# One addition on VectorE, moved behind a tile's lower parts in one step of each unit

## The chip, the core and the metric

The kernel runs on one core of a Trainium2 chip. TensorE (PE, with its weight loads shown as PEld) multiplies and transposes, VectorE (DVE), ScalarE (ACT) and GpSimd (POOL) work beside it, and SyncE (SP) issues the transfers. Each engine takes its instructions in the order of its own queue and waits for others by semaphores. The metric is the device time of one execution in microseconds, lower is better.

## The reference

Attention with a threshold, then two matrix products with a softplus between them. Eight batches, eight heads, 576 rows, head width 64; 4608 rows of 512 for the second half.

```python
scale = 1.0 / np.sqrt(q.shape[-1])
scores = scale * np.matmul(q, k.transpose(0, 1, 3, 2))
thresh = np.max(scores, axis=-1, keepdims=True) - tau
scores = np.where(scores >= thresh, scores, -1000000000.0)
scores = scores - np.max(scores, axis=-1, keepdims=True)
attn = np.exp(scores)
attn = attn / (np.sum(attn, axis=-1, keepdims=True) + 1e-09)
out = np.matmul(attn, v)
...
h = x @ w_in
g = np.maximum(h, 0.0) + np.log1p(np.exp(-np.abs(h)))
return g @ w_out
```

## The kernel before

**Units and tiles.** Attention is done in 32 units, each a batch and a pair of heads, and a unit in nine tiles of 128 query rows (the middle one holds the last 64 rows of both heads). Tiles are counted through, so tile 72 is the first of unit 8, and `now["tile"] % 9` is a tile's place in its unit.

**One tile.** PE makes the scores `s` (L442). DVE takes the negated row maximum `negm` and a threshold `thr`. ACT takes the exponential into `e_all`. DVE masks it (SCALAR_TENSOR_TENSOR on `e_all`, with a row sum). PE transposes the weights back into the bank of the scores (L490, L493, L496). The values are to be multiplied in two parts, so ACT copies the transposed weights as upper parts `gH`, and DVE subtracts these from the bank for the lower parts: `gL` and, for the rest of the rows, `gH` on half the partitions. There are two score banks, used in turn. The scores of a tile can be written when the lower parts of the tile two before it have been taken out of their bank.

**Values.** After some tiles a group of columns is complete, and `values` multiplies it on PE (L574 to L576) into a bank `pv`: upper parts of the values give one half of its partitions, lower parts the other. One step later `values_out` adds the halves: ACT copies one half into `xp`, and DVE adds the other to it (TENSOR_TENSOR `xp<-pv,xp`). There are four groups in a unit; the one of 320 columns that is called at place 5 is the second.

**The other stream.** Beside the attention runs the second half of the reference for rows that are finished: products with the first matrix (`h`, L664 to L668), softplus on ACT, its split into parts on DVE (CAST `g<-st`) and POOL, products with the second (`o`, L732), and their sum into `acc` by ACT or DVE. Keys and queries of the next unit are transposed on PE too (`tr`, L375 to L383).

**Banks.** `h`, `o`, `pv`, `tr` and a few others share one pool of four PSUM banks, `ps_g` (`GB = 4`). A product gets a bank once what was read from it before has been read.

**What sets the order.** A list of steps for each tile, `PAT = "ThRlefmpfxSvwp"`: T transposes the weights of the tile, h and l are its upper and lower parts, R, e and m the next tile's maximum, exponential and mask, f a share of the other stream, x values and the next unit's transposes, S the scores of the tile after next. At p whatever was deferred is called, the additions of `values_out` among it. From tile 72 on (`TQ`) each instruction that goes to DVE or ACT through `vec` and `act` is tied behind the one before it, so these two queues have exactly the order in which the code calls them; line L156 is the helper through which they all go. The other queues are ordered by the scheduler of the framework.

Of the kernel before, what the change touches and what calls it, by code (L numbers as in the profile page):

```python
# [13 lines left out]
ALU = mybir.AluOpType  # L14
# [38 lines left out]
TQ = 72  # L53
# [7 lines left out]
def tile_kernel(ctx: ExitStack, tc: tile.TileContext, q, k, v, tau, w_in, w_out, out):  # L61
# [70 lines left out]
    def lo_of(eng, out_, in_, hi):  # L132
        eng.tensor_tensor(out=out_, in0=in_, in1=hi.bitcast(F32), op=ALU.subtract)  # L133
# [4 lines left out]

    now = {"p": 0, "tile": 0}
    masked = []  # L140
    scored = []

    def behind(i, others):
# [19 lines left out]
    vec = Queue(nc.vector)  # L163
# [282 lines left out]
    def row_max(s, t):  # L446
        negm = apool.tile([P, 1], F32, tag="negm", bufs=3, name=f"negm_{s.i}_{t}")
        thr = apool.tile([P, 1], F32, tag="thr", bufs=3, name=f"thr_{s.i}_{t}")
        vec.reduce_max(negm, s.sp[t][:, :, 0:HS], axis=AX.XY, negate=True)
        vec.tensor_scalar(out=thr, in0=negm, scalar1=-1.0, scalar2=ntau, op0=ALU.mult, op1=ALU.add)  # L450
        s.m[t] = (negm, thr)

    def exps(s, t):
        act.activation(e_all[:, s.half[t], :].rearrange("p (h n) -> p h n", h=2), s.sp[t][:, :, 0:HS],
                             AF.Exp, bias=s.m[t][0], scale=1.0)

    def mask(s, t):
        e2 = e_all[:, s.half[t], :].rearrange("p (h n) -> p h n", h=2)
        masked.append(vec.scalar_tensor_tensor(
            out=e2, in0=s.sp[t][:, :, 0:HS], scalar=s.m.pop(t)[1], in1=e2, op0=ALU.is_ge, op1=ALU.mult,  # L460
            accum_out=s.sums[:, s.tiles.index(t):s.tiles.index(t) + 1]))

    def group(s, g):
        if g not in s.grp:
            h = apool.tile([P, NC + 1, 320], F32R, tag="gH", name=f"gH_{s.i}_{g}")
            l = None if s.whole else apool.tile([P, NC, 320], F32R, tag="gL", name=f"gL_{s.i}_{g}")
            s.grp[g] = (h, l)
        return s.grp[g]
# [8 lines left out]
    def weights_T(s, t):  # L477
        half = s.half[t]
        e = e_all[:, half, :]
        other, second = mate(s, t)  # L480
        lone = other is None
        if 9 * NPAIR * s.b + 9 * s.hp + t < TG:
            main = ps_g.tile([P, NC, P], F32, tag="g", name=f"tm_{s.i}_{t}")
            rest = ps_g.tile([P, NC, P], F32, tag="g", name=f"tr_{s.i}_{t}")[:, 0, :] if lone or second else None
        else:
            sp = s.sp[t]
            main = sp[:, 0, :].rearrange("p (c n) -> p c n", n=P)
            rest = sp[:, 1, 0:P]
        if second:
            nc.tensor.transpose(rest, e_all.rearrange("p h n -> p (h n)")[:, SM:SM + P], ident)  # L490
        for c in range(NC):
            c0 = half * SR + c * P
            nc.tensor.matmul(main[:, c, :], e[:, c0:c0 + P], ident, is_transpose=True, start=True, stop=True)  # L493
        if lone:
            r0 = 0 if half else SM
            nc.tensor.transpose(rest[0:SR, :], e[:, r0:r0 + SR], ident)  # L496
        s.sp[t] = (main, rest)

    def rests(s, t):

        lo, hi = slice(0, SR), slice(SR, P)
        other, second = mate(s, t)
        if other is None:
            return [(t, lo, lo, hi)]
        if not second:
            return []
        return [(x, (lo, hi)[s.half[x]], (lo, hi)[s.half[x]], (hi, lo)[s.half[x]]) for x in (other, t)]
# [4 lines left out]
    def weights_hi(s, t):  # L512
        main, rest = s.sp[t]
        for g, c0, s0, n in s.place[t]:
            h = group(s, g)[0]
            h = h.bitcast(F32) if s.whole else h
            act.copy(h[:, 0:NC, c0:c0 + n], main[:, :, s0:s0 + n])
        both = rests(s, t)
        if len(both) == 2 and not s.whole:

            (g, c0, _, n), = s.place[both[0][0]]
            act.copy(group(s, g)[0][:, NC, c0:c0 + 2 * n].rearrange("p (k n) -> p k n", k=2),
                           rest.unsqueeze(1).to_broadcast([P, 2, n]))
            return
        for x, rows, up, down in both:
            for g, c0, s0, n in s.place[x]:
                h = group(s, g)[0][:, NC, c0:c0 + n]
                if not s.whole:
                    act.copy(h[up], rest[rows, s0:s0 + n])
                elif len(both) == 2:  # L530
                    act.activation(h.bitcast(F32), rest, AF.Copy, scale=side[:, s.half[x]:s.half[x] + 1])
                else:
                    act.copy(h[up].bitcast(F32), rest[rows, s0:s0 + n])
                    nc.gpsimd.memset(h[down].bitcast(F32), 0.0)

    def weights_lo(s, t):
        main, rest = s.sp.pop(t)
        if s.whole:
            return
        for g, c0, s0, n in s.place[t]:  # L540
            h, l = group(s, g)
            lo_of(vec, l[:, :, c0:c0 + n], main[:, :, s0:s0 + n], h[:, 0:NC, c0:c0 + n])
        for x, rows, up, down in rests(s, t):
            for g, c0, s0, n in s.place[x]:
                h = group(s, g)[0]
                lo_of(vec, h[down, NC, c0:c0 + n], rest[rows, s0:s0 + n], h[up, NC, c0:c0 + n])
# [4 lines left out]
    def slow_products():  # L551
        if not slow:
            return
        for f in slow[0][:3]:
            behind(f(), scored)
        del slow[0][:3]
        if not slow[0]:
            slow.pop(0)
            defer(1, ends.pop(0))
# [19 lines left out]
    def values_out(s, g, o):  # L579
        j, x0, n, _ = s.groups[g]  # L580
        keep = slice(j * D, (j + 1) * D)
        move = slice((1 - j) * D, (2 - j) * D)
        xs = s.xp[keep, x0:x0 + n]
        act.copy(xs, o[move, 0:n])
        vec.tensor_tensor(out=xs, in0=o[keep, 0:n], in1=xs, op=ALU.add)

    def row_scales(s):
        nt = len(s.tiles)
# [245 lines left out]
    def point():  # L834
        now["p"] += 1
        due = [x for x in later if x[0] <= now["p"]]
        later[:] = [x for x in later if x[0] > now["p"]]
        for _, f in due:
            f()
# [10 lines left out]
    while sum(u.T for u in chunks) < NT:  # L850
# [4 lines left out]
        b, o = divmod(u.t0 + u.T - 1, S)  # L855
# [5 lines left out]
    def target(g):  # L861

        done = 0
        for n, u in enumerate(chunks):
            work = 3 * NFC * (NCC * u.T / 512 + u.T / P)
            end = first[n + 1] if n + 1 < len(chunks) else 1 << 30
            if g < end:
                rate = work / (end - first[n])
                if n + 2 >= len(chunks) or end == first[n]:
                    rate = NMM  # L870
                return done + max(0, min(work, (g - first[n]) * rate))
            done += work
        return done

    prep = []
    for kind, g in WL:
        for m in range(4):
            n = len(prep)
# [84 lines left out]
    for g, (cur, t) in enumerate(tiles):  # L963
        now["tile"] = g
        t9 = cur.tiles.index(t) + 1
        even = g + 1 if cur.kind != "all" else g + 1 - t9 + 9 * sum(Q9[:t9]) / sum(Q9)
        quota = target(even) - done
        nxt = tiles[g + 1] if g + 1 < NS else None
        upto = done
        for step in PAT0 + ("m" if g == TG - 1 else "") if g < TG else PAT:  # L970
            if step == "T":
                weights_T(cur, t)
            elif step == "h":
                weights_hi(cur, t)
            elif step == "l":
                weights_lo(cur, t)
            elif step == "R" and nxt:
                row_max(*nxt)
            elif step == "e" and nxt:
                exps(*nxt)  # L980
            elif step == "m" and nxt:
                mask(*nxt)
            elif step == "M":
                mask(cur, t)
            elif step == "f":
                upto += quota / PAT.count("f")
                while done < upto:
                    done += next(ffn)
            elif step == "x":
                extras(cur.i, cur.tiles.index(t))  # L990
            elif step == "S" and g + 2 < NS:
                scores(*tiles[g + 2])
            elif step == "v":
                slow_products()
            elif step == "w":
                while prep and prep[0][0] <= g:
                    _, f, a = prep.pop(0)
                    f(*a)
            elif step == "p":
                point()  # L1000
# [39 lines left out]
```

## Time and profile before

| | |
|---|---|
| median of 3 runs | 1426.15 us (1426.09 to 1426.85) |
| the profiled execution | 1425.26 us |
| its span, first to last instruction | 1423.5 us |
| its mean granted TensorE clock | 1.000 |
| additions `xp<-pv,xp` of 64x320 on DVE | 54, mean 485 ns |
| additions `xp<-pv,xp` of 64x256 on DVE | 54, mean 421 ns |

A row of the timeline has the start in us, the length in us, the engine, the line, the operation, what it writes and reads, the shape and how many equal instructions it joins; in brackets stand the idle time of the engine just before it and what ended that. A row of waits has the waiting engine and line, what it waited for, the total in us, how often, and the longest.

### The profile page before, as it was taken

The numbers are of one execution on the slowest core, as the hardware profiler recorded it, in microseconds if no ns is written. First come the engines' busy times: TensorE is split into PE (matmuls) and PEld (weight loads), VectorE is DVE, ScalarE is ACT, GpSimd is POOL, SyncE is SP. The second block draws the span as 40 slices with busy tenths as digits, with TensorE's granted clock in tenths as the row PEclk, the third lists the DMA queues.
The fourth block names the chain that finished last, engine by engine and source line by source line (L and its number), as shares of the span: only waits on it lengthen the run. The fifth ranks groups of instructions, "written<-read, shape, count | busy, mean of one in ns | idle before, by whom it ended". The sixth has DMA issues, their size and how long they took to land.

```text
span 1423.5 us, 23587 instructions
## 1 busy us (share of the span) xinstructions
PE 1380.4 (97%) x7860; PEld 1164.5 (82%) x7860; DVE 987.5 (69%) x2211; ACT 846.7 (59%) x1615; POOL 586.2 (41%) x619
## 2 busy tenths in 40 slices
PE   6987999999999999999999999999999999999998
PEld 5555688788888888888888888888888888788886
DVE  6988688787777777787778777877777777402111
ACT  5766767667666576667666666667666765221110
POOL 3666666543333433344334333344334431323221
PEclk9999999999999999999999999999999999999999
DMA  5766766435333534445443533453434532343421
GB/s 168 220 191 208 233 195 186 125 102 173 111 105 111 156 105 124 120 131 158 118 119 98 158 108 110 124 145 117 123 113 141 154 94 84 110 130 115 135 76 45
DMA packets 131209, 189.94 MB, mean 133 GB/s; under 512 B 35312, under 2 KB 86800, under 8 KB 131088
## 3 DMA queue, kind: packets, MB, share of 16 engines
q1 hardware_dynamic: 131088, 188.43, 45.4%
q8 instruction: 63, 1.03, 0.3%
q14 instruction: 58, 0.48, 0.1%
HBM read 140.51 MB, written 27.41 MB: 118 GB/s over the span
## 4 chain that ended last, share of the span: by engine, by line
PE 86%; DVE 4%; DMA 2%; issue 2%; POOL 2%; ACT 1%; SPq 1%; POOLq 0%; DVEq 0%; ACTq 0%
PE o L732 28%; PE s L442 11%; PE h L664 9%; PE h L666 9%; PE h L668 9%; PE s L493 7%; PE pv L574 4%; PE pv L575 4%; PE tr L383 2%; DVE e_all L156 1%; PE pv L576 1%; DVE negm L156 1%; PE s L490 1%; PE pv L568 1%; DMA wc_i<-in_moe_w_in_dram 1%
## 5 line engine op out<-in xcount | busy, mean ns | idle before, releaser
L732 PE MATMUL o<-wo_o,g 128*128 128x512 f32 x1728 | 446.4, 400 | 1.1 <-POOL g L133 1.1
L732 PEld LDWEIGHTS o<-wo_o,g 128*128 128x128 f32 x1728 | 313.7, 189 | 60.6 <-POOL g L133 2.1
L133 POOL TENSOR_TENSOR g<-st,g 128x512 fp32r<-128x512 f32 x144 | 189.8, 1338 | 240.4 <-DVE g L156 222.4
L156 DVE SCALAR_TENSOR_TENSOR e_all<-s,thr,e_all 128x576 f32<-128x576 f32 x288 | 235.2, 817 | 38.0 <-ACT e_all L156 33.4
L156 ACT CAST gH<-s 128x512 fp32r<-128x512 f32 (+2 forms) x432 | 179.5, 467 | 136.8 <-PE s L493 115.5
L156 ACT ACTIVATE e_all<-s,negm 128x576 f32<-128x576 f32 x288 | 215.8, 750 | 32.7 <-DVE negm L156 17.0
L664 PE MATMUL h<-xh,wi 128*128 128x512 f32 x576 | 232.6, 404 | 1.8 <-ACT xh L156 0.8
L156 DVE TENSOR_REDUCE negm<-s 128x1 f32<-128x576 f32 x288 | 215.2, 747 | 25.0 <-PE s L442 21.9
L666 PE MATMUL h<-xl,wi 128*128 128x512 f32 x576 | 231.6, 402 | 0.7 <-POOL xl L133 0.7
L668 PE MATMUL h<-xh,wi 128*128 128x512 f32 x576 | 229.2, 398 | 0.0
L156 DVE TENSOR_TENSOR gL<-s,gH 128x512 fp32r<-128x512 f32 (+1 forms) x270 | 169.0, 634 | 47.3 <-ACT gH L156 40.5
L442 PE MATMUL s<-kT,qT 128*128 128x288 f32 x1024 | 193.0, 311 | 8.1 <-ACT gH L156 4.1
L156 DVE CAST g<-st 128x512 fp32r<-128x512 f32 x128 | 58.8, 501 | 169.0 <-ACT st L156 169.0
L442 PEld LDWEIGHTS s<-kT,qT 128*128 128x128 f32 x1024 | 148.4, 191 | 24.6 <-ACT gH L156 5.3
L493 PE MATMUL s<-identr,e_all 128*128 128x128 f32 x1008 | 151.3, 273 | 0.2 <-DVE e_all L156 0.2
L156 ACT ACT_TABLE_LOAD x111 | 142.4, 1283 | 5.4 <-PE h L668 3.4
L156 ACT ACTIVATE st<-h 128x512 f32<-128x512 f32 x144 | 78.3, 595 | 112.5 <-PE h L668 111.8
L664 PEld LDWEIGHTS h<-xh,wi 128*128 128x128 f32 x576 | 108.5, 188 | 25.7 <-ACT xh L156 1.3
L493 PEld LDWEIGHTS s<-identr,e_all 128*128 128x128 f32 x1008 | 119.4, 140 | 10.9 <-DVE e_all L156 3.5
L666 PEld LDWEIGHTS h<-xl,wi 128*128 128x128 f32 x576 | 108.6, 188 | 22.2 <-POOL xl L133 1.5
L668 PEld LDWEIGHTS h<-xh,wi 128*128 128x128 f32 x576 | 108.5, 188 | 22.1
L574 PE MATMUL pv<-gH,vt 128*128 128x256 f32 (+1 forms) x432 | 118.3, 297 | 0.3 <-ACT gH L156 0.2
(94 smaller groups left out, 1830.0 us busy)
## 6 DMA issues: line engine op xcount, KB each, us to landing
wi<-wi_d SPq DMA_DIRECT2D x144, 512.0 KB
qT<-qT SPq DMA_DIRECT2D x124, 128.0 KB
R<-r_d SPq DMA_DIRECT2D x64, 144.0 KB
kn<-in_k_dram SPq DMA_DIRECT2D x32, 256.0 KB
qn<-in_q_dram SPq DMA_DIRECT2D x32, 256.0 KB
vn<-in_v_dram SPq DMA_DIRECT2D x32, 256.0 KB
wc_i<-in_moe_w_in_dram SPq DMA_DIRECT2D x16, 512.0 KB
wi_d<-wc_i SPq DMA_DIRECT2D x32, 256.0 KB
```

Source lines behind the costliest of these rows:

```text
L133: eng.tensor_tensor(out=out_, in0=in_, in1=hi.bitcast(F32), op=ALU.subtract)
L156: i = getattr(self.eng, name)(*args, **kwargs)
L383: nc.tensor.transpose(pr[:, c * P:(c + 1) * P], src, identr)
L442: i = nc.tensor.matmul(sp[:, hf, 0:HS], lhs, s.kT[j][:, k0 + hf * HS:k0 + (hf + 1) * HS], start=(m == 0), stop=(m == len(parts) - 1))
L490: nc.tensor.transpose(rest, e_all.rearrange("p h n -> p (h n)")[:, SM:SM + P], ident)
L493: nc.tensor.matmul(main[:, c, :], e[:, c0:c0 + P], ident, is_transpose=True, start=True, stop=True)
L574: nc.tensor.matmul(o[:, 0:n], vt[:, c, :], h[:, c, 0:n], start=(c == 0), stop=False)
L575: nc.tensor.matmul(o[:, 0:n], vt[:, c, :], l[:, c, 0:n], start=False, stop=False)
L664: nc.tensor.matmul(h, wi[:, 0, cc, :], u.h[cc], start=(cc == 0), stop=False)
L666: nc.tensor.matmul(h, wi[:, 0, cc, :], u.l[cc], start=False, stop=False)
L668: nc.tensor.matmul(h, wi[:, 1, cc, :], u.h[cc], start=False, stop=(cc == NCC - 1))
L732: nc.tensor.matmul(o, u.g[fc][m // 2][:, sl], wo[fc][:, m % 2, :], start=(n == 0), stop=(n == 3 * QF - 1))
```

## The change

From tile 72 on, at the tile at place 5 of each unit, the addition of `values_out` is kept in a list instead of being called at the p that ends the tile. It is called in the next tile, right behind its lower parts. ACT's copy stays where it was.

```diff
+    put_off = []
...
         act.copy(xs, o[move, 0:n])
-        vec.tensor_tensor(out=xs, in0=o[keep, 0:n], in1=xs, op=ALU.add)
+        add = lambda: vec.tensor_tensor(out=xs, in0=o[keep, 0:n], in1=xs, op=ALU.add)
+
+        if now["tile"] >= TQ and now["tile"] % 9 == 5:
+            put_off.append(add)
+        else:
+            add()
...
                 weights_lo(cur, t)
+                while put_off:
+                    put_off.pop(0)()
```

Lines below the new list are numbered one higher in the changed kernel, and higher still further down: L156 is L157 there, L383 is L384, L442 is L443, L493 is L494, L732 is L738.

DVE in unit 18, from the casts at the end of the tile at place 5 to the sum into `acc` behind the next mask. `negm_18_7` is the maximum of the tile at place 7, `gL_18_2` and `gH_18_2` are the lower parts of the tile at place 6, and the row that ends in 128x576 is the mask. Before:

```order
L156 CAST g0_3_8_8385<-st_3_8_8358 128x512 [waits Activation_49]
L156 CAST g0_3_9_8389<-st_3_9_8356 128x512 [waits Pool_49]
L156 TENSOR_TENSOR xp_18_8194<-pv_18_1_8365,xp_18_8194 64x320 [waits Activation_49]
L156 TENSOR_REDUCE negm_18_7_8402<-s_1_143 128x1 [waits PE_49]
L156 TENSOR_SCALAR thr_18_7_8403<-negm_18_7_8402,ntau_85 128x1 [waits DVE_49]
L156 TENSOR_TENSOR gL_18_2_8280<-s_0_142,gH_18_2_8279 128x4x128 [waits PE_49,Activation_49]
L156 TENSOR_TENSOR gH_18_2_8279<-s_0_142,gH_18_2_8279 64x128 x2
L156 SCALAR_TENSOR_TENSOR e_all_141,sums_18_8020<-s_1_143,thr_18_7_8403,e_all_141 128x576 [waits DVE_49,Activation_49]
L156 TENSOR_TENSOR acc_3_0_7984<-o_3_1_0_8360,acc_3_0_7984 128x512 [waits DMAHW5_49,DMAHW4_49,PE_49]
```

and in the changed kernel:

```order
L157 CAST g0_3_8_8385<-st_3_8_8358 128x512 [waits Activation_49]
L157 CAST g0_3_9_8389<-st_3_9_8356 128x512 [waits Pool_49]
L157 TENSOR_REDUCE negm_18_7_8401<-s_1_143 128x1 [waits PE_49]
L157 TENSOR_SCALAR thr_18_7_8402<-negm_18_7_8401,ntau_85 128x1 [waits DVE_49]
L157 TENSOR_TENSOR gL_18_2_8280<-s_0_142,gH_18_2_8279 128x4x128 [waits PE_49,Activation_49]
L157 TENSOR_TENSOR gH_18_2_8279<-s_0_142,gH_18_2_8279 64x128 x2
L157 TENSOR_TENSOR xp_18_8194<-pv_18_1_8365,xp_18_8194 64x320
L157 SCALAR_TENSOR_TENSOR e_all_141,sums_18_8020<-s_1_143,thr_18_7_8402,e_all_141 128x576 [waits DVE_49,Activation_49]
L157 TENSOR_TENSOR acc_3_0_7984<-o_3_1_0_8360,acc_3_0_7984 128x512 [waits DMAHW5_49,DMAHW4_49,PE_49]
```

The addition has moved past the maximum, the threshold and three instructions of lower parts, and stands in front of the mask.

PE at the same place, from a product of the other stream (`o_3_1_1`) over the transposes of the next unit's keys (`tr_19_1_0`) and queries (`tr_19_1_1`) and the scores of the tile at place 8 (`s_0`) to the weight transposes of the tile at place 7 (L493). Before:

```order
L732 MATMUL o_3_1_1_8419<-wo_o5_1509,g0_3_5_7931 128x512 x2
L383 MATMUL tr_19_1_0_8425<-identr_81,k2_19_8154 128x128 [waits Activation_49]
L383 MATMUL tr_19_1_0_8425<-identr_81,k2_19_8154 128x128 x3
L383 MATMUL tr_19_1_1_8431<-identr_81,q2_19_1_8378 128x128 [waits DVE_49,Pool_49]
L383 MATMUL tr_19_1_1_8431<-identr_81,q2_19_1_8378 128x128 x3
L442 MATMUL s_0_142<-kT_18_1_7972,qT0_18_1_7978 128x288 [waits DVE_49,Activation_49]
L442 MATMUL s_0_142<-kT_18_1_7972,qT0_18_1_7978 128x288
L442 MATMUL s_0_142<-kT_18_1_7972,qT1_18_1_7979 128x288 x2
L732 MATMUL o_3_1_1_8419<-wo_o5_1509,g1_3_5_7932 128x512
L732 MATMUL o_3_1_1_8419<-wo_o6_1584,g0_3_6_8264 128x512
L493 MATMUL s_1_143<-identr_81,e_all_141 128x128 [waits DVE_49]
L493 MATMUL s_1_143<-identr_81,e_all_141 128x128 x3
```

and in the changed kernel:

```order
L738 MATMUL o_3_1_1_8419<-wo_o5_1509,g0_3_5_7931 128x512 x2
L384 MATMUL tr_19_1_0_8425<-identr_81,k2_19_8154 128x128 [waits Activation_49]
L384 MATMUL tr_19_1_0_8425<-identr_81,k2_19_8154 128x128 x3
L384 MATMUL tr_19_1_1_8431<-identr_81,q2_19_1_8378 128x128 [waits DVE_49,Activation_49,Pool_49]
L384 MATMUL tr_19_1_1_8431<-identr_81,q2_19_1_8378 128x128 x3
L443 MATMUL s_0_142<-kT_18_1_7972,qT0_18_1_7978 128x288 [waits Activation_49]
L443 MATMUL s_0_142<-kT_18_1_7972,qT0_18_1_7978 128x288
L443 MATMUL s_0_142<-kT_18_1_7972,qT1_18_1_7979 128x288 x2
L494 MATMUL s_1_143<-identr_81,e_all_141 128x128 [waits DVE_49]
L494 MATMUL s_1_143<-identr_81,e_all_141 128x128 x3
L738 MATMUL o_3_1_1_8419<-wo_o5_1509,g1_3_5_7932 128x512
L738 MATMUL o_3_1_1_8419<-wo_o6_1584,g0_3_6_8264 128x512 x2
```

The scheduler has put the weight transposes two products earlier, right behind the scores. The wait for DVE has gone from the scores; the query transposes, in front of them, wait for DVE in both, and for ACT as well now. The same move by two products is found in 17 of the 24 units: in 11 of them no product is left between the scores and the weight transposes, in six one is. In six units PE's order is as it was, and in the last unit, where no next keys and queries are transposed, the scores and the weight transposes come earlier too.

## The prediction

> **What bounds the kernel now.** I read the page first: its busy shares, then its chain of work that ended last.
>
> ```profile
> PE 1380.4 (97%) x7860; PEld 1164.5 (82%) x7860; DVE 987.5 (69%) x2211; ACT 846.7 (59%) x1615; POOL 586.2 (41%) x619
> PE 86%; DVE 4%; DMA 2%; issue 2%; POOL 2%; ACT 1%; SPq 1%; POOLq 0%; DVEq 0%; ACTq 0%
> ```
>
> TensorE is busy 97% of the span and carries 86% of the chain; VectorE (DVE) carries 4%. The change works from tile 72 on, in the last 24 of 32 units. The view of busy time by stretch gives a part of them (PE, weight loads, DVE, ACT, POOL, clock, DMA), and the view of waits for the weight loads from 330 to 1230 us the longest wait there:
>
> ```profile
> 390.00:600.00 210.00, 209.64 (x1262) 184.40 (x1261) 163.65 (x374) 138.98 (x257) 80.49 (x86) 1.00 0.43 122
> PEld s L442 <- issue: 3.1, 17, 0.2
> ```
>
> PE is busy 209.64 of 210 us at a granted clock of 1.00, so nothing is left to hide a delay of PE, and every wait put into PE's queue lengthens the run by its own length. What can still be won is small: one kind of wait, 17 times 0.2 us, ahead of the scores (L442). So the question for a DVE reorder is only which PE instruction waits for which DVE instruction.
>
> **The change, step by step.** The timeline of unit 18 shows the place; PE, DVE and ACT rows in order of start:
>
> ```profile
> 704.47 1.36 DVE L156 CAST g<-st 128x512 fp32r<-128x512 f32 x2 [1.57 <-ACT st L156]
> ...
> 705.75 0.47 DVE L156 TENSOR_TENSOR xp<-pv,xp 64x320 f32<-64x320 f32 x1
> 705.79 1.28 ACT L156 ACT_TABLE_LOAD   x1
> 706.15 0.74 DVE L156 TENSOR_REDUCE negm<-s 128x1 f32<-128x576 f32 x1
> ...
> 707.05 0.68 DVE L156 TENSOR_TENSOR gL<-s,gH 128x512 fp32r<-128x512 f32 x1
> 707.09 0.74 ACT L156 ACTIVATE e_all<-s,negm 128x576 f32<-128x576 f32 x1
> ...
> 707.75 0.59 DVE L156 TENSOR_TENSOR gH<-s,gH 64x128 fp32r<-64x128 f32 x2
> 707.87 0.40 PEld L383 LDWEIGHTS tr<-identr,q 128*128 128x128 f32 x4
> 707.90 0.51 PE L383 MATMUL tr<-identr,q 128*128 128x128 f32 x4
> 708.37 0.82 DVE L156 SCALAR_TENSOR_TENSOR e_all<-s,thr,e_all 128x576 f32<-128x576 f32 x1
> 708.45 0.56 PEld L442 LDWEIGHTS s<-kT,qT 128*128 128x128 f32 x4 [0.19 <-issue]
> 708.48 0.76 PE L442 MATMUL s<-kT,qT 128*128 128x288 f32 x4
> ...
> 709.08 0.63 PE L732 MATMUL o<-wo_o,g 128*128 128x512 f32 x2
> 709.11 0.08 DVE L156 DVE_READ_ACCUMULATOR e_all<-s,thr,e_all 128x1 f32 x1
> 709.11 0.69 DVE L156 TENSOR_TENSOR acc<-o,acc 128x512 f32<-128x512 f32 x1
> 709.28 0.59 ACT L156 CAST kT<-tr 128x512 fp32r<-128x512 f32 x1 [1.45 <-PE s L442]
> 709.32 0.59 PEld L493 LDWEIGHTS s<-identr,e_all 128*128 128x128 f32 x4
> 709.55 0.60 PE L493 MATMUL s<-identr,e_all 128*128 128x128 f32 x4
> ```
>
> The addition (705.75) stands between two casts and the row maximum; from the first cast to the mask (708.37) DVE idles nowhere. The scores at 708.45 follow the lower parts, which end at 707.75 + 0.59 = 708.34: this is the wait of 0.2 us.
>
> *Removed in front.* The maximum started 0.40 us after the addition (705.75 to 706.15), so it, the threshold and the lower parts come 0.40 us earlier. The lower parts then end at 707.94. ACT's exponential does not move: it starts at 707.09, when its table load (705.79 + 1.28) is over, and ends at 707.83.
>
> *Added behind.* The mask began 0.03 us after the lower parts ended; taking the same gap, the addition runs from 707.97 to 708.44, and the mask 0.40 us after its start, at 708.37, where it was. For the mask and all that follows on DVE the change is a wash. The addition issues no DMA; in SP's queue a store and a load change places at five points, and no transfer is among the waits of PE in this stretch.
>
> The Trainium skill's page "VectorE: DVE Perf Modes", section "The DRAIN you can't avoid", has the next DVE instruction start when the one before it has left the pipeline. The trace differs for this addition: it ends at 706.22, and the maximum starts at 706.15. The same page's section "Two Vector instructions with no wait between them" makes a start early or late by the quarter of the partitions where the operands begin, and by it the addition is held behind the lower parts and the mask is not held behind the addition, as I took it above. By the first rule alone the lower parts would gain 0.47 instead of 0.40 us and the sum below would be 17 x 0.07 = 1.2 us smaller.
>
> *What waits for the addition.* It is the instruction that empties the PSUM bank of the value product. Its pool has four banks. When PE reaches the query transposes (707.87) one bank holds a product whose sum into acc comes only at 709.11, one holds the product under way, one the key transposes, copied out only at 709.28. So the query transposes must take the bank of the value product. The PE rows in the section on the change agree: these transposes wait for DVE in both programs, and in the changed one the scores behind them no longer do, since an earlier wait on DVE's count already covers the lower parts. That earlier wait can only be for something behind the lower parts and in front of the mask: the addition. Before, it ended at 706.22, 1.65 us in time; now it ends at 708.44.
>
> The price of this new wait: from the end of the lower parts (708.34) to the load that waited for it (708.45) there were 0.11 us, and 0.03 more to the matmul. So the load comes at 708.55 and the first query transpose at 708.58 instead of 707.90: **0.68 us later**. Queued behind it on PE are the scores, the transposes of the weights and all products.
>
> *What is given back.* A unit without casts shows the pace when nothing waits:
>
> ```profile
> 627.28 0.86 ACT L156 CAST gH<-s 128x512 fp32r<-128x512 f32 x2 [0.65 <-PE s L493]
> ...
> 628.17 0.69 DVE L156 TENSOR_TENSOR gL<-s,gH 128x512 fp32r<-128x512 f32 x1
> ...
> 628.88 0.59 DVE L156 TENSOR_TENSOR gH<-s,gH 64x128 fp32r<-64x128 f32 x2
> ...
> 629.50 0.82 DVE L156 SCALAR_TENSOR_TENSOR e_all<-s,thr,e_all 128x576 f32<-128x576 f32 x1
> ...
> 630.33 0.40 PEld L383 LDWEIGHTS tr<-identr,q 128*128 128x128 f32 x4
> 630.36 0.51 PE L383 MATMUL tr<-identr,q 128*128 128x128 f32 x4
> ...
> 630.71 0.77 PE L442 MATMUL s<-kT,qT 128*128 128x288 f32 x4
> 631.18 0.49 PEld L493 LDWEIGHTS s<-identr,e_all 128*128 128x128 f32 x4
> 631.32 0.60 PE L493 MATMUL s<-identr,e_all 128*128 128x128 f32 x4
> ```
>
> Here the scores follow the first query transpose by 0.35 us (630.36 to 630.71); in unit 18 it was 0.58 (707.90 to 708.48). The old wait of 0.23 us disappears, as the lower parts are done earlier. Net: 0.68 - 0.23 = **0.45 us per unit**.
>
> *The moved weight transposes.* In the 17 units with casts PE now issues the four weight transposes (L493) two products earlier. Two products cost PE the same on either side, so this is worth nothing unless the transposes have to wait for the mask. Without a wait they come 0.61 us after the scores (630.71 to 631.32): 708.93 + 0.61 = 709.54. The mask is through at 709.19 and its signal there at 709.30, so the new wait ahead covers this one. If it did not, the price is that of rival A.
>
> *The six units without casts* (unit 16 above is one): the lower parts wait for ACT's upper parts (627.28 + 0.86 = 628.14), so they gain nothing, and the addition goes to 629.50 to 629.97. Its signal, at 630.08, is 0.25 us ahead of the load at 630.33. The mask moves 0.40 us, to an end at 630.72 and a signal at 630.83; its transposes load at 631.18. Cost nothing; with that cover gone, at most 0.40 us each, 2.4 us. The last unit has no next queries and exchanges one wait for a like one: nothing.
>
> *The sum.* 17 x 0.45 = 7.7 us; the count is that of the old wait, 17, which is also the number of units whose PE order changes in this way. PE has no slack to absorb it. The profiled execution took 1425.26 us for its span of 1423.5; with 7.7 us it becomes 1433.0. The median of the runs shown is 0.89 us above it, so I forecast **1433.9 us**, 0.5% slower.
>
> *Bounds of the price.* If the bank is free 0.07 us before the addition's end (the overlap at 706.15), 0.38 us per unit, 6.5 us in all. If the third semaphore that the query transposes now wait for takes another 0.11 us, 0.56 us per unit and 9.5 us; with the six other units hit too, 11.9 us. I take 0.45, worked out from the row nearest to the case, a PE load that waited for DVE.
>
> **Rivals.**
> A, the bank comes free in time. Then only the moved weight transposes count: the old wait goes (scores at 708.25), the transposes would start at 708.86 but the mask's signal comes at 709.30 and the matmul at 709.33: a wait of 0.47 for one of 0.23 saved, 0.24 us in the 11 units where no product is left between scores and transposes. In six units one is left, about 0.23 us long (two start at 709.08, the transposes at 709.55), and the two waits balance. 11 x 0.24 = 2.6 us, 1428.8. For it: four banks with a free one could exist at another moment. Against: the changed wait lists.
> B, **faster**: the old wait goes in 17 units and nothing replaces it, 17 x 0.23 = 3.9 us less, 1422.2. The place is DVE between casts and mask. It needs the addition to end by 707.76 (the load at 707.87 less 0.11), and the mask as much earlier, so the chain from cast to mask would have to be 0.68 us shorter when the addition leaves the front. Against it: that chain has no idle time, and the same instructions stay in it.
> C, more than forecast: the other units wait as well, +11.9 us, 1438.1.
> D, DVE's order changes and nothing on PE notices: 1426.2.
>
> **Chances.** Forecast 0.78 (own range 1432.6 to 1435.7), C 0.07, A 0.06, B 0.05, D 0.04. The range, 1431 to 1438, holds the first two. About 0.2%, 2.9 us, is what a measurement of this kernel can tell from no change. Slower by more: 0.78 + 0.07 and a sliver of A, 0.86; within it: A and D, 0.09; faster: B, 0.05.
>
> **What the changed profile would show.** If I am right: a wait of PE's weight loads ahead of the query transposes (L384 then), about 0.6 to 0.7 us, 17 times; the addition back to back with the lower parts; no wait ahead of the scores; masks and exponentials in their old places; units with casts 0.45 us longer, the others unchanged. Query transposes on time with the weight transposes late would be A; neither late, B or D. I would be wrong if the bank were signalled before the addition is over, or if PE recovered the delay somewhere in the same unit, where I see no idle time to recover it from.

## The result and the profile after

| | before | changed |
|---|---|---|
| median, 6 runs each | 1427.03 us (1426.09 to 1430.54) | 1437.38 us (1433.55 to 1441.15) |
| profiled execution, its span | 1425.26 us, 1423.5 us | 1438.44 us, 1436.7 us |
| its granted clock | 1.000 | 0.997 |

The changed kernel is slower, ratio 1.0068 with an interval of 1.0047 to 1.0088. The forecast was 1433.9 us in a range of 1431 to 1438.

The page of the changed kernel, busy shares and chain by engine:

```profile
PE 1384.2 (96%) x7860; PEld 1167.6 (81%) x7860; DVE 987.2 (69%) x2211; ACT 846.6 (59%) x1615; POOL 586.4 (41%) x619
PE 81%; DVE 6%; ACT 4%; DMA 4%; issue 3%; POOL 2%; SPq 1%; POOLq 0%; ACTq 0%; DVEq 0%
```

The busy times of DVE and ACT are those of before within 0.3 us, so no work was added. PE's share of the chain fell from 86% to 81%; the engines that it waits for took the difference. The busy time by stretch, and the waits of the weight loads and of PE itself from 330 to 1240 us:

```profile
390.00:600.00 210.00, 207.41 (x1250) 182.40 (x1249) 161.55 (x372) 139.41 (x258) 82.97 (x89) 1.00 0.43 124
PEld tr L384 <- POOL g L133: 10.7, 17, 0.6
PEld s L443 <- issue: 0.4, 1, 0.4
PE tr L384 <- DVE xp L157: 5.7, 11, 0.5
PE tr L384 <- ACT acc L157: 3.1, 6, 0.5
```

PE now idles 2.59 us in a stretch in which it idled 0.36. The 17 waits of 0.2 us ahead of the scores have gone; 17 waits of 0.63 us (10.7 / 17) stand ahead of the query transposes (`tr`, L384). The releasers in these rows differ (POOL, DVE, ACT), because a wait for several semaphores is put down to one that came late; which one holds is settled by the experiments. Unit 18, PE, DVE and ACT in order of start:

```profile
710.10 1.35 DVE L157 CAST g<-st 128x512 fp32r<-128x512 f32 x2 [1.57 <-ACT st L157]
...
711.38 0.74 DVE L157 TENSOR_REDUCE negm<-s 128x1 f32<-128x576 f32 x1
...
712.29 0.68 DVE L157 TENSOR_TENSOR gL<-s,gH 128x512 fp32r<-128x512 f32 x1
712.71 0.74 ACT L157 ACTIVATE e_all<-s,negm 128x576 f32<-128x576 f32 x1
712.99 0.59 DVE L157 TENSOR_TENSOR gH<-s,gH 64x128 fp32r<-64x128 f32 x2
...
713.59 0.48 DVE L157 TENSOR_TENSOR xp<-pv,xp 64x320 f32<-64x320 f32 x1
714.00 0.80 DVE L157 SCALAR_TENSOR_TENSOR e_all<-s,thr,e_all 128x576 f32<-128x576 f32 x1
714.19 0.39 PEld L384 LDWEIGHTS tr<-identr,q 128*128 128x128 f32 x4 [0.63 <-POOL g L133]
714.22 0.51 PE L384 MATMUL tr<-identr,q 128*128 128x128 f32 x4 [0.52 <-DVE xp L157]
714.53 0.56 PEld L443 LDWEIGHTS s<-kT,qT 128*128 128x128 f32 x4
714.56 0.76 PE L443 MATMUL s<-kT,qT 128*128 128x288 f32 x4
...
715.03 0.49 PEld L494 LDWEIGHTS s<-identr,e_all 128*128 128x128 f32 x4
715.16 0.60 PE L494 MATMUL s<-identr,e_all 128*128 128x128 f32 x4
```

The addition is back to back with the lower parts, and ends at 714.07; 0.12 us later comes the load for the query transposes. Everything behind it on PE follows without a wait.

To see how much of the run this is, the start of a unit's first mask serves as a mark. Units 8 and 31, before, then changed:

```profile
293.26 0.82 DVE L156 SCALAR_TENSOR_TENSOR e_all<-s,thr,e_all 128x576 f32<-128x576 f32 x1
...
1181.27 0.82 DVE L156 SCALAR_TENSOR_TENSOR e_all<-s,thr,e_all 128x576 f32<-128x576 f32 x1
```

```profile
295.92 0.82 DVE L157 SCALAR_TENSOR_TENSOR e_all<-s,thr,e_all 128x576 f32<-128x576 f32 x1
...
1191.21 0.82 DVE L157 SCALAR_TENSOR_TENSOR e_all<-s,thr,e_all 128x576 f32<-128x576 f32 x1
```

The middle, between these marks, took 888.01 us before (1181.27 - 293.26) and 895.29 us after (1191.21 - 295.92): 7.28 us more. Unit by unit, by the same marks, the 17 units with casts in this stretch are each 0.41 to 0.46 us longer, and the six without casts are unchanged within 0.02 us. Of the other 5.9 us between the two profiled spans, 2.66 us came ahead of unit 8, where nothing was changed, and 3.2 us from the first mask of unit 31 on.

### The profile page after: what moved, and what is told of

Read it like the earlier page. It is cut to its first block, busy times and chain, and to the rows that moved or that the text cites. A ratio compares the mean times of both kernels' runs of the same rounds, so it can differ in the third digit from the quotient of the medians.

```text
span 1436.7 us, 23565 instructions
## 1 busy us (share of the span) xinstructions
PE 1384.2 (96%) x7860; PEld 1167.6 (81%) x7860; DVE 987.2 (69%) x2211; ACT 846.6 (59%) x1615; POOL 586.4 (41%) x619
## 4 chain that ended last, share of the span: by engine, by line
PE 81%; DVE 6%; ACT 4%; DMA 4%; issue 3%; POOL 2%; SPq 1%; POOLq 0%; ACTq 0%; DVEq 0%
PE o L738 24%; PE s L443 11%; PE h L670 9%; PE h L672 9%; PE h L674 9%; PE s L494 7%; PE pv L575 4%; PE pv L576 4%; PE tr L384 2%; DVE e_all L157 1%; PE pv L569 1%; DMA wc_o<-in_moe_w_out_dram 1%; DMA wi<-wi_d 1%; ACT e_all L157 1%; DVE negm L157 1%
## 5 line engine op out<-in xcount | busy, mean ns | idle before, releaser
L738 PE MATMUL o<-wo_o,g 128*128 128x512 f32 x1728 | 446.1, 401 | 2.7 <-POOL g L133 2.7
L738 PEld LDWEIGHTS o<-wo_o,g 128*128 128x128 f32 x1728 | 315.5, 189 | 63.9 <-POOL g L133 3.7
L157 DVE SCALAR_TENSOR_TENSOR e_all<-s,thr,e_all 128x576 f32<-128x576 f32 x288 | 234.7, 815 | 38.5 <-ACT e_all L157 35.0
L157 ACT CAST gH<-s 128x512 fp32r<-128x512 f32 (+2 forms) x432 | 179.4, 467 | 133.6 <-PE s L494 112.8
L157 DVE TENSOR_REDUCE negm<-s 128x1 f32<-128x576 f32 x288 | 215.4, 748 | 32.8 <-PE s L443 29.9
L157 ACT ACTIVATE e_all<-s,negm 128x576 f32<-128x576 f32 x288 | 216.1, 751 | 35.5 <-PE tr L491 16.4
L157 DVE TENSOR_TENSOR gL<-s,gH 128x512 fp32r<-128x512 f32 (+1 forms) x270 | 168.8, 634 | 53.4 <-ACT gH L157 45.7
L443 PE MATMUL s<-kT,qT 128*128 128x288 f32 x1024 | 193.0, 311 | 6.5 <-ACT gH L157 3.7
L157 DVE CAST g<-st 128x512 fp32r<-128x512 f32 x128 | 57.6, 491 | 169.3 <-ACT st L157 169.3
L443 PEld LDWEIGHTS s<-kT,qT 128*128 128x128 f32 x1024 | 148.7, 191 | 20.4 <-ACT gH L157 4.9
L494 PE MATMUL s<-identr,e_all 128*128 128x128 f32 x1008 | 151.4, 273 | 0.3 <-DVE e_all L157 0.2
L157 ACT ACTIVATE st<-h 128x512 f32<-128x512 f32 x144 | 78.2, 596 | 113.8 <-PE h L674 113.2
L494 PEld LDWEIGHTS s<-identr,e_all 128*128 128x128 f32 x1008 | 119.3, 140 | 9.1 <-DVE e_all L157 3.5
```

What stands on the lines that cost most here:

```text
L157: i = getattr(self.eng, name)(*args, **kwargs)
L443: i = nc.tensor.matmul(sp[:, hf, 0:HS], lhs, s.kT[j][:, k0 + hf * HS:k0 + (hf + 1) * HS], start=(m == 0), stop=(m == len(parts) - 1))
L738: nc.tensor.matmul(o, u.g[fc][m // 2][:, sl], wo[fc][:, m % 2, :], start=(n == 0), stop=(n == 3 * QF - 1))
```

## The experiments

Each is a whole kernel. "Middle" is the time between the two marks above, read from its own profile.

**The change again.**

> The changed kernel once more, for its spread. Bank theory: in 17 units the query transposes wait about 0.6 us for the addition and the old wait ahead of the scores (0.23 us) is gone, 0.43 us per unit, 7.3 us in all; runs at full granted clock are 7 to 8 us above the kernel before at full clock, and whatever is above that goes with stretches of half clock, in which the mean granted clock is under 1.000. Rival, the change itself costs more than 7.3 us (10 us or more): then runs at a granted clock of 1.000 are that much longer too.

Median 1436.3 us, ratio 1.0072 (1.0055 to 1.0089). The middle took 895.23 us, 0.06 us from the first profile. Of the twelve timed runs of the changed kernel three had a granted clock of 0.999 or more; their mean, 1434.3 us, is 8.0 us above the mean of such runs of the kernel before (1426.4 us, 14 of the 52 timed beside the experiments). That is the 7 to 8 us expected; the rival's 10 us do not show.

**The addition behind the maximum.** One piece of the move alone: behind the maximum and the threshold, in front of the lower parts.

```diff
                 row_max(*nxt)
+                while put_off:
+                    put_off.pop(0)()
...
                 weights_lo(cur, t)
-                while put_off:
-                    put_off.pop(0)()
```

> The addition stands behind the next maximum and its threshold, but in front of the lower parts. PE's order has the weight transposes two products earlier, as in the changed kernel. Bank theory: the addition ends about 1 us earlier than in the changed kernel (near 707.0 on the scale of unit 18), before the query transposes need the bank at 707.9, so their wait is gone; the old wait ahead of the scores is back (0.23 us, 17 times), and in 11 units the weight transposes wait some 0.2 us for the mask: +2 to +3 us against the kernel before, 1428 to 1430. Rival, putting the addition off behind the maximum costs by itself or the new PE order does: +7 us or more, as in the changed kernel.

Median 1429.63 us, ratio 1.0024 (1.0010 to 1.0037); the middle took 890.34 us, 2.3 more than before. In unit 18:

```profile
706.09 0.47 DVE L157 TENSOR_TENSOR xp<-pv,xp 64x320 f32<-64x320 f32 x1
...
707.30 0.40 PEld L384 LDWEIGHTS tr<-identr,q 128*128 128x128 f32 x4
...
707.88 0.56 PEld L443 LDWEIGHTS s<-kT,qT 128*128 128x128 f32 x4 [0.18 <-issue]
...
708.68 0.42 PEld L494 LDWEIGHTS s<-identr,e_all 128*128 128x128 f32 x4 [0.23 <-DVE e_all L157]
```

With the addition over at 706.56, the query transposes wait for nothing, and the old wait of the scores is back. What is left is the wait of the weight transposes for the mask, 11 times 0.21 us in the marks: the scheduler has put them two products earlier, as in the changed kernel, and here the wait ahead of them is too short to cover theirs.

**ACT empties the bank.** DVE's order stays that of the changed kernel, but ACT copies the second half out of the bank too, and DVE adds the two copies.

```diff
-        add = lambda: vec.tensor_tensor(out=xs, in0=o[keep, 0:n], in1=xs, op=ALU.add)
...
-            put_off.append(add)
+            half = apool.tile([P, S], F32, tag="R", bufs=1, name=f"half_{s.i}_{g}")[keep, 0:n]
+            act.copy(half, o[keep, 0:n])
+            put_off.append(lambda: vec.tensor_tensor(out=xs, in0=half, in1=xs, op=ALU.add))
```

> As the changed kernel, but ACT copies both halves of the product out of the bank and DVE adds the two copies behind the lower parts: DVE's and PE's order are those of the changed kernel, only the bank is free as soon as ACT is done. Bank theory: no wait ahead of the query transposes and none ahead of the scores; in 11 units the weight transposes wait for the mask, 0.2 us net, in six nothing is lost or gained: +1 to +3 us, 1427 to 1429. Rival, DVE's new order costs whatever the bank does: +7 us. Rival B of the prediction, nothing replaces the old wait: -3.9 us, 1422.

Median 1435.74 us, ratio 1.0066 (1.0051 to 1.0080), 6.7 us above the 1429 us that the theory had given at most. The middle took 897.60 us. Its unit 18:

```profile
709.95 2.66 POOL L133 TENSOR_TENSOR g<-st,g 128x512 fp32r<-128x512 f32 x2 [0.36 <-DVE g L157]
...
711.75 0.74 ACT L157 ACTIVATE e_all<-s,negm 128x576 f32<-128x576 f32 x1
...
712.24 0.40 PEld L384 LDWEIGHTS tr<-identr,q 128*128 128x128 f32 x4
...
712.35 0.60 DVE L157 TENSOR_TENSOR xp<-half,xp 64x320 f32<-64x320 f32 x1
...
712.88 0.80 DVE L157 SCALAR_TENSOR_TENSOR e_all<-s,thr,e_all 128x576 f32<-128x576 f32 x1
...
713.75 0.42 PEld L494 LDWEIGHTS s<-identr,e_all 128*128 128x128 f32 x4 [0.60 <-DVE e_all L157]
```

This run tells the releasers apart. The query transposes load at 712.24, before the addition starts (712.35) and while POOL's parts still run (709.95 + 2.66 = 712.61): so they wait neither for POOL nor for the addition as such, only for the bank to be empty. But the time did not come back. ACT's second copy stands ahead of the exponential, the addition from two copies takes 0.60 us instead of 0.48 (it ends 0.34 us after POOL's parts), and the mask comes behind both: it starts at 712.88, 0.39 us after the exponential's end (712.49). Now the weight transposes wait, 0.60 us. The expectation left out that the mask is the next wall: in the changed kernel it ends at 714.80 and, 0.12 us from end to load, allows the load of the weight transposes at 714.92, where they come at 715.03. Only 0.1 us of the bank's wait could be won before theirs begins. This is rival A's mechanism, but the middle grew by 9.6 us where rival A had 2.6. The 17 units with casts make 6.1 of them. The other 3.5 us come from the six units without casts, which this kernel does not leave alone: there the addition takes 1.50 us beside another instruction of POOL, and the weight transposes wait 0.55 us or more for the mask. So this run shows what the query transposes wait for, but not what an earlier bank alone would be worth.

**Only the casts moved.** The addition stays where it was before; instead the two casts of the other stream (with POOL's parts) go behind the lower parts.

```diff
-                parts_of(u, fc, t)
+                if TQ <= now["tile"] < NS and now["tile"] % 9 == 5 and u.n:
+                    put_off.append(lambda fc=fc, t=t: parts_of(u, fc, t))
+                else:
+                    parts_of(u, fc, t)
...
                 weights_lo(cur, t)
+                while put_off:
+                    put_off.pop(0)()
```

> The addition stays in front; instead the two casts of the other stream (and POOL's lower parts of them) are put behind the tile's lower parts at the same place. DVE then no longer waits 1.57 us for softplus in front of them. Theory, PE pays for every wait and for nothing else: lower parts are done near 707.5, the query transposes find their bank free, the scores do not wait (-0.23 us in 17 units), the mask ends a little earlier than before and the weight transposes, one product earlier in 11 units, do not wait: -3 to -4 us, 1422 to 1423. Rival, POOL's parts come 2 us later and products wait for them: no gain or a loss.

Median 1425.73 us, ratio 0.9988 (0.9977 to 0.9999), 1.6 us below before where 3 to 4 were expected. The middle took 886.47 us, 1.5 less than before. The waits of the weight loads, 330 to 1240 us:

```profile
PEld s L494 <- DVE e_all L157: 6.0, 22, 0.4
PEld o L736 <- POOL g L133: 1.9, 2, 1.0
PEld s L443 <- issue: 0.5, 1, 0.5
```

The old wait is gone, but the casts in front of the mask make the weight transposes wait for it, 5.1 us in the 17 units (the other five of the 22 waits, 0.9 us, stand in the units without casts, and before as well). By difference, about 2.4 of the 3.9 us of the old wait (17 x 0.23) are lost to it. DVE had idled 2.02 us ahead of the addition for ACT's copy while the maximum could have run.

**The addition behind the mask.** One place further back than the change has it.

```diff
                 mask(*nxt)
+                while put_off:
+                    put_off.pop(0)()
...
                 weights_lo(cur, t)
-                while put_off:
-                    put_off.pop(0)()
```

> The addition goes one place further back, behind the mask; PE's order answers by putting the query transposes behind the scores and, in 11 of the 17 units with casts, behind two products and two weight transposes. Bank theory (the loss is the wait of the query transposes for the bank that the addition empties): in unit 18 the mask would start at 707.97 and the addition end about 709.3, and PE has the scores and two products to do until then, so the waits of 0.63 us ahead of the query transposes go or shrink below 0.3 us: 1425 to 1430 us, 5 to 10 us less than with the change. Rival (what costs is that DVE does the addition late, whoever waits): the addition is later still, so at least as slow as with the change: 1436 us or more.

Median 1431.25 us, ratio 1.0028 (1.0018 to 1.0039): a miss by 1.25 us for the bank theory's range, and 5 us below the rival's. The addition is later still and the kernel is faster than the changed one, since PE has other work meanwhile; unit 18:

```profile
714.71 0.48 DVE L157 TENSOR_TENSOR xp<-pv,xp 64x320 f32<-64x320 f32 x1
714.88 0.59 ACT L157 CAST kT<-tr 128x512 fp32r<-128x512 f32 x1 [1.07 <-PE s L443]
...
715.58 0.39 PEld L384 LDWEIGHTS tr<-identr,q 128*128 128x128 f32 x4 [0.29 <-issue]
```

The query transposes wait 0.29 us at their new place, until 0.11 us after ACT's copy of the key transposes ends (715.47), not after the addition (715.19). The middle took 891.48 us, 3.5 more than before: eleven of the 17 units are 0.20 to 0.24 us longer. So are the six units without casts, by 0.21 to 0.36 us, which cost nothing with the change. There the query transposes stand between two pairs of scores, and in unit 16 they load at 636.67, 0.11 us after the end of the addition (636.08 + 0.48): again a wait for the bank.

**Maximum, addition, lower parts, casts.** The second and the fourth experiment put together: in the tile behind place 5 the addition follows the maximum and the threshold, and the casts follow the lower parts.

> The row maximum and threshold first, then the addition, then the lower parts, then the two casts (with their POOL parts), then the mask. Bank theory: the addition ends about 2 us ahead of the query transposes, the lower parts in time for the scores, the mask within 0.1 us of the end of the exponential; no wait ahead of query transposes or scores, and less than the 6.0 us ahead of the weight transposes that stood where only the casts were moved: 2 to 4 us below before, 1423 to 1425. Rival (DVE's chain from cast to mask sets the unit whatever its order): same as before, 1426 to 1428.

Median 1425.66 us, ratio 0.9983 (0.9973 to 0.9993), 0.66 us above the range expected; the middle took 885.40 us, 2.6 less than before. Its longest kinds of wait on weight loads, 330 to 1240 us:

```profile
PEld s L495 <- DVE e_all L158: 2.4, 11, 0.3
PEld o L742 <- POOL g L133: 2.2, 2, 1.1
```

Of 17 units 11 gain 0.20 to 0.26 us, the old wait; in the other six it turned into a wait for the mask of about the same length (the other five of the 11 waits stand in units without casts, as before). By the middle the rival (no order of DVE makes a difference) falls; the time, 0.34 us below its range, would not settle it. It is the fastest middle of all, but the whole gain is at the edge of what can be measured.

**The change, with the casts behind it.** The addition stands behind the lower parts, as changed, and the casts behind the addition.

```diff
-                parts_of(u, fc, t)
+                if TQ <= now["tile"] < NS and now["tile"] % 9 == 5 and u.n:
+                    casts.append(lambda fc=fc, t=t: parts_of(u, fc, t))
+                else:
+                    parts_of(u, fc, t)
...
                 while put_off:
                     put_off.pop(0)()
+                while casts:
+                    casts.pop(0)()
```

> The change as it is, the addition behind the lower parts, but the two casts put behind the addition. Bank theory: position behind the lower parts is harmless when the lower parts come early: the addition would end about 0.4 us ahead of the query transposes, so the 17 waits of 0.63 us go; the mask stands where it stood when only the casts were moved: 1424 to 1427, 9 to 12 us less than with the change. Rival (the place behind the lower parts is what costs, by the hold in DVE's pipeline or by the mask): 1433 us or more.

Median 1430.96 us, ratio 1.0026 (1.0016 to 1.0035). Unit 18 on DVE, and the waits of weight loads, 330 to 1240 us:

```profile
709.98 0.69 DVE L158 TENSOR_TENSOR gL<-s,gH 128x512 fp32r<-128x512 f32 x1 [0.52 <-ACT gH L158]
710.68 0.59 DVE L158 TENSOR_TENSOR gH<-s,gH 64x128 fp32r<-64x128 f32 x2
711.28 0.48 DVE L158 TENSOR_TENSOR xp<-pv,xp 64x320 f32<-64x320 f32 x1
711.69 0.74 DVE L158 CAST g<-st 128x512 fp32r<-128x512 f32 x2
```

```profile
PEld s L495 <- DVE e_all L158: 6.6, 22, 0.4
PEld o L742 <- POOL g L133: 3.3, 2, 2.2
```

The place behind the lower parts, with the same neighbour in front, costs no wait of the query transposes once the lower parts themselves come early: all 17 are gone. Of the 6.6 us ahead of the weight transposes 5.7 stand in the 17 units, the rest elsewhere, as before. The middle took 889.69 us, 1.7 more than before and 5.6 less than changed, and the time is 2 us below the rival's. The time was expected at 1427 at most; about 2 of the 4 us by which it is missed lie outside the middle, and the second row of waits shows where: the wait for POOL at the end of the run that is described next.

**Start and end of the run.** Kernels without any edit, once each, for the parts that the change does not touch: the kernel before twice, and the changed one twice more.

> The kernel before, unchanged, for the spread of the parts of a run that the change does not touch. From the mask of unit 8 to that of unit 31 it should take the 888.0 us of the first profile within 0.1 us (the way of the change's 7.3 us); the stretch up to unit 8 and the stretch behind the last mask may each differ by 1 to 3 us, if the 2 to 3 us by which the timed difference exceeds 7.3 are the spread of those parts. If both stretches repeat within 0.3 us, the excess belongs to the change.

> As the run beside it: 888.0 us from unit 8 to unit 31 within 0.1 us; the stretches ahead and behind differ by 1 to 3 us if they are spread.

> The changed kernel once more, for its start and its end. From unit 8 to unit 31 895.2 to 895.3 us as twice already. If the 2 to 3 us beyond 7.3 belong to the change, the end behind the last mask is 210 us or more, as in one of two profiles (211.25 and 208.24; before 207.66 to 208.00 in three); if they are spread, it is 208 to 209.

> As the run beside it: 895.2 to 895.3 us in the middle; an end of 210 us or more if the excess belongs to the change, of 208 to 209 us if it is spread.

With the profiles above that makes three of before and four of the change:

| | up to unit 8 | middle | from unit 31 on |
|---|---|---|---|
| before | 293.3, 294.7, 295.1 | 888.0, 887.9, 888.1 | 242.2, 242.5, 242.2 |
| changed | 295.9, 294.6, 297.5, 293.2 | 895.3, 895.2, 895.3, 895.4 | 245.4, 242.4, 243.8, 243.8 |

The middle repeats within 0.2 us in both (0.1 was expected), so the 7.3 us are sure. The start is spread: 1.8 us between profiles of before, 4.3 between those of the change. The end is not only that. Behind the last mask the two new profiles of the change took 209.57 and 209.64 us, between the bounds that had been set for the two theories; but before repeated within 0.35 us (207.66 to 208.00), and from unit 31 on three of four profiles of the change are at least 1.2 us longer than any of before. The waits of PE from 1215 us on, before and changed, first profile of each:

```profile
PE o L732 <- POOL g L133: 1.1, 2, 0.7
```

```profile
PE o L738 <- POOL g L133: 2.7, 2, 2.0
```

In the three long ones this wait is 2.6 to 2.7 us, in the fourth 1.4, in the three of before 1.1 to 1.5. POOL is late there because its scaling of the last values waits longer for a transfer, before and changed:

```profile
1228.18 1.47 POOL L612 TENSOR_TENSOR xp<-xp,R 128x576 f32<-128x576 f32 x1 [16.04 <-DMA R<-r_d]
```

```profile
1239.89 1.41 POOL L618 TENSOR_TENSOR xp<-xp,R 128x576 f32<-128x576 f32 x1 [17.83 <-DMA wi<-wi_d]
```

The row scales `R` share the queues with weights (`wi`) of 512 KB that are loaded right behind them. From the issue of `R` to the scaling it is 5.5 to 5.6 us in the three long ones, 4.1 in the fourth and 3.8 to 4.1 in those of before. The longer wait of PE goes with a late addition: it stands in five of the six profiles of kernels whose addition reads the bank behind the lower parts or the mask (2.4 to 2.7 us), and in none of the seven others (1.0 to 1.5). So this part most likely belongs to the change; why `R` comes later was not tried and stays open.

## Why the prediction was right

Unit 18 runs 5.63 us later in the changed profile (the casts start at 710.10 instead of 704.47). With that added, the times forecast stand beside those measured:

| step | forecast | measured |
|---|---|---|
| lower parts end | 713.57 | 713.58 |
| addition starts | 713.60 | 713.59 |
| mask starts | 714.00 | 714.00 |
| load of the query transposes | 714.18 | 714.19 |
| query transposes | 714.21 | 714.22 |
| scores | 714.56 | 714.56 |
| weight transposes | 715.17 | 715.16 |

- *Removed in front and added behind.* The lower parts came 0.40 us earlier and the mask kept its place, as forecast. The addition started 0.01 us after the lower parts' end, and the mask 0.07 us before the addition's end (714.00 against 713.59 + 0.48). That is the pattern which the Trainium skill's page "VectorE: DVE Perf Modes", section "Two Vector instructions with no wait between them", gives; by the rule at the head of its section "The DRAIN you can't avoid" alone, to which that section names the former as the exception, the mask would have started no earlier than 714.07, and the trace shows the exception.
- *What waits for the addition.* The query transposes wait for the bank of the value product. Two runs show it from both sides: empty the bank earlier by moving the addition up, or by another engine, and the 17 waits go, while POOL's parts still run. With the casts behind the addition they go too, at the changed place.
- *The net price.* Forecast 0.68 - 0.23 = 0.45 us a unit and 7.7 us in all; measured 7.28 / 17 = 0.43 and 7.3. The six units without casts cost nothing, as forecast; the last unit, put down at nothing too, is 0.3 to 0.4 us shorter between its first and last mask.
- *The moved weight transposes.* Covered, as forecast: no wait stands ahead of them in the 17 units of the changed kernel. They do cost where no earlier wait covers them, 11 times 0.21 us with the addition behind the maximum; rival A had priced this at 11 times 0.24.
- *The sum.* This is the term that was too small: 1433.9 us forecast, 1437.38 and 1436.3 measured, both above the forecast's own range of 1432.6 to 1435.7. That they lie inside 1431 to 1438 is owed to the room left for rival C. About 1 us of it is the base: the forecast added 7.7 us to 1426.15, the median of three runs, and the medians of 6, 23 and 29 runs of the kernel before were 1427.03, 1427.32 and 1427.22 us. Another part is the end, which was put down at nothing, and no transfer was seen among the waits: from unit 31 on it was 1.2 us or more longer in three of four profiles. What is then left is no larger than the spread of the start, and times go with the clock: of the changed kernel's two times six runs the three at a clock of 0.999 or more took 1433.55, 1434.43 and 1435.01 us, and the slowest, 1441.15, had 0.994. That the half-clock stretches below make up this remainder was not tested.

Rival C's time, 1438.1, came close to the median, but its mechanism, waits in the units without casts, did not occur. Rival B's 3.9 us were there to be had only in part, and by another order: 2.6 us.

## What to carry to other kernels

An instruction that empties a PSUM bank is late when the next user of that bank comes up in PE's queue, not when its own result is needed: before moving it, count the bank's ring and find that user. Where PE is busy 97%, a wait of 0.6 us (0.43 net of the one that it replaces) that recurs in 17 places is 0.5% of the run, and clearing it uncovers the next wait, here that for the mask, which stood 0.1 us behind. To judge half a per cent, measure between two marks inside the run: the middle repeated within 0.2 us where whole runs spread by up to 8.

## What the runs showed of the hardware

*Half clock after a gap in PE's work.* Two pairs of neighbouring stretches of the changed profile (behind the stretch and its length stands PE's busy time; the granted clock is the third number from the end):

```profile
83.80:87.20 3.40, 1.10 (x11) 0.85 (x10) 2.33 (x6) 3.40 (x12) 2.90 (x4) 1.00 0.43 160
87.24:90.64 3.40, 3.40 (x11) 1.92 (x9) 2.66 (x6) 1.37 (x3) 3.23 (x4) 0.50 0.45 108
1240.90:1244.30 3.40, 0.99 (x3) 0.65 (x4) 0.00 (x0) 0.00 (x0) 3.40 (x4) 1.00 0.37 87
1244.36:1247.76 3.40, 3.40 (x9) 2.63 (x8) 0.66 (x1) 0.00 (x0) 1.86 (x2) 0.50 0.35 86
```

After 3.4 us in which PE was busy for 1.10 or 0.99 us, the clock was 0.50 for the next 3.4 us. The second of these follows the long wait at the end of the run, so such a wait can cost more than its own length; half of 3.4 us, 1.7 us, is an estimate for one stretch from these rows. Behind the last mask this profile took 211.25 us, and the two others with the same long wait, which have no such stretch there, 209.57 and 209.64: 1.6 us less. The Trainium skill's page "TensorE: Matmul & The Clock Gate", Part 1, ties the half rate to an idle window of about 3.4 us; the length agrees, but here the window ahead was a third busy. In the profile of the change again it was half busy (1.67 us of the 3.41 from 82.99 us on), and 0.50 followed all the same. The profile of before, with a mean clock of 1.000, has none ahead of its last microsecond.

*A DVE instruction that starts during one of POOL can last until that has ended.* The casts `g<-st`, 390 to 1180 us, in the kernel before and in the one with the casts behind the addition:

```profile
L156 DVE CAST g<-st 128x512 fp32r<-128x512 f32 x82 | 39.7, 525 | 50.8 <-ACT st L156 50.8
```

```profile
L158 DVE CAST g<-st 128x512 fp32r<-128x512 f32 x82 | 31.0, 418 | 25.7 <-ACT st L158 25.7
```

The same 82 casts took 525 ns each in the one and 418 ns in the other, 8.7 us of DVE time in all. The difference lies in 16 casts of the kernel before, each the first of a pair: they start while POOL is already splitting the values, take 0.79 to 1.02 us and end 0.28 us after POOL's instruction. The 41 casts that overlap POOL's parts `g` start ahead of these and take 418 ns; the 25 with nothing beside them on POOL take 427. The addition from two copies, where ACT empties the bank, does as the 16 do: started during an instruction of POOL, it ends 0.34 us after it, 0.60 or 1.50 us long. So in these rows it counts which of the two starts first; no run moved POOL's work alone.
